# Second batch's first stage moved from the prologue into the unit loop

## The chip, the cores and the metric

The kernel runs on one core of one Trainium2 chip. The metric is the device time of one execution in microseconds. TensorE (PE in the rows) multiplies, VectorE (DVE), ScalarE (ACT) and GpSimd (POOL) work element by element, and SyncE (SP) issues most of the DMAs. Each engine takes its instructions strictly in the order of the program, and SP's queue does so too: a DMA that waits there holds back every DMA behind it.

## The reference

```python
def _attn_ref(x, w_r, w_i, b_r, b_i):            # x: 8 x 3072 x 256
    X = np.fft.rfft(x, axis=1)
    Yr = Xr @ w_r - Xi @ w_i + b_r
    Yi = Xr @ w_i + Xi @ w_r + b_i
    ...                                          # soft threshold by 0.01 of both
    return np.fft.irfft(Y, n=x.shape[1], axis=1)

def reference(**kwargs):
    x = _attn_ref(...).reshape(B * S, D)         # 24576 x 256
    x = _moe_ref(x, w_in, w_out)                 # relu(x @ w_in) ** 2 @ w_out
    return _moe2_ref(x, phi, w1, w2)             # 32 slots, 8 experts
```

The change touches the first part alone: the Fourier transform along the sequence, the complex product with the weights, the threshold and the way back.

## The kernel before

A sequence of 3072 is cut as 48 x 64, so that each transform becomes small matrix products. For each of the 8 batches there are two kinds of work.

The **first stage** of a batch is four blocks (`NA = 4`), numbered j over all batches: j = 0 to 3 are batch 0, j = 4 to 7 batch 1, and so on to 31. `a_mm(j, q)` (L214) multiplies two tiles of x (chunks 2j and 2j+1, each loaded by `load_x`, L204, in two DMAs of 192 KB) into four PSUM banks `psA`. `a_out` (L227, L232) copies one bank to SBUF, and after every second copy stores the result to a DRAM tensor `ad` of the batch in two DMAs. Copies not yet made stand in the list `done`.

The **units** are u = 0 to 95, twelve in each batch. `load_b(u)` (L239) reads rows of `ad` for units u and u+1 with two DMAs. As these rows cut across all blocks of the batch, the first one of a batch waits until every store of its four blocks has landed. Then come `b_mm` (`psB`, L247), the splits into high and low parts (`b_hi`, `b_lo`, `b_sum`), `l_mm` (`psL` and `psS`, L117 to L119, the weights' products), `l_move`, `l_relu`, `l_soft` on VectorE and ScalarE, and for two units together `c_mm` (`psC`, L331) and `c_out`, which stores to `zd`.

The units are software-pipelined by one loop over half units h: unit u's `b_mm` stands at h = 2u, its `l_mm` at h = 2(u+2), its `c_mm` at h = 2(u+4)+1. The function `starts(j)` gives the h at which block j's products are put in; at the other h one waiting `a_out` is made. At odd units `load_b(U+3)` is issued, so the first load of batch b stands at h = 24b - 5 and its first product at h = 24b.

Ahead of the loop stands the prologue: the loads of x for batch 0, the weights, the bias (`bias[0]`, read by `l_move`), block j = 0 to 3 and in this kernel one block more (`EX = 1`, j = 4), then 12 products on zeros (`busy1`, L503), `load_b(0)`, `load_b(2)` and the split of the weights. A decoder of weights that are stored in 64 bits (`decode`, L363 to L395) runs step by step from h = 17 on; each step of it on VectorE waits for a tile `raw` that SP has loaded.

At most eight DMAs of SP and ScalarE are on their way at once: each takes one of eight semaphores (DMAHW0 to 7) in turn, and waits for the DMA that had it before.

Of the kernel before, what the change touches and what calls it, by code (L numbers as in the profile page):

```python
# [25 lines left out]
DM = 256  # L26
NF = 16
TB = 8
NC = N2 // TB
# [74 lines left out]
def fft_moe_kernel(ctx, tc, x, w_r, w_i, b_r, b_i, moe_w_in, moe_w_out, moe2_phi, moe2_w1, moe2_w2,  # L104
                   c_f1, c_bm, c_cm, c_dm, c_st, out):
    nc = tc.nc
    NB = x.shape[0]
# [3 lines left out]
    NU = NP // 2  # L111
# [9 lines left out]
    def split(hi, lo, v, eng=None):  # L121
        nc.scalar.copy(hi, v)  # L122
        (eng or nc.vector).tensor_tensor(out=lo, in0=v, in1=f(hi), op=ALU.subtract)  # L123

    def drain(it):
        for _ in it:
            pass
# [31 lines left out]
    def early(tag, name):  # L159

        if tag.startswith("wia"):
            t = f(wpool.tile([128, 4, 2, 128], F32R, tag=tag, name=name).rearrange("p a b n -> p (a b n)"))
        else:
            t = wg[:, int(tag[2:])]
        return t.rearrange("p (a d) -> p a d", d=DM)
# [10 lines left out]
    bias = [k1p.tile([128, 2, DM], F32, tag=f"bias{j}", name=f"bias{j}") for j in range(2)]  # L176
# [7 lines left out]
    NA = N2 // 16  # L184
# [6 lines left out]
    def load_x(c):  # L191
        if c >= XL or c in xt:
            return
        b, k = divmod(c, NC)
        if c < NC:
            t = early(f"wia{c}", f"xt{c}")
        else:
            t = wka.tile([128, TX, DM], F32, tag="xt", name=f"xt{c}", bufs=XB)
        xv = x[b].rearrange("(n1 n2) d -> n1 n2 d", n2=N2)
        m = TX // 2 if c == 0 else TX  # L200
        for o in range(0, TX, m):
            for r in range(2):
                n = 16 * (k // 2) + 8 * r + 4 * (k % 2) + o
                nc.sync.dma_start(t[64 * r:64 * r + N1, o:o + m], xv[:, n:n + m])  # L204
        xt[c] = t

    def a_mm(j, q):
        b = j // NA
        if b not in ad:
            ad[b] = dram.tile([N1, N2, DM], F32, tag="ad", name=f"ad{b}", bufs=3)  # L210
        ps = [pbank(f"psA{j}_{q}_{r}").rearrange("p (a d) -> p a d", a=2) for r in range(2)]
        for r in range(2):
            for c in range(2):
                nc.tensor.matmul(ps[r][64 * c:64 * c + 64], lhsT=f1t[64 * r:64 * r + N1],  # L214
                                 rhs=xt[2 * j + c][64 * r:64 * r + N1, 2 * q:2 * q + 2], start=True, stop=True)
        for r in range(2):
            pa[j, q, r] = ps[r]
        if q:
            xt.pop(2 * j)
            xt.pop(2 * j + 1)  # L220

    def a_out(j, q, r, copy):
        i = 2 * j + r
        b, k = divmod(i, 2 * NA)
        if q == 0:
            sa[i] = early(f"wo{k}", f"sa{i}") if b == 0 else wka.tile([128, TX, DM], F32, tag="sa", name=f"sa{i}")
        copy(sa[i][:, 2 * q:2 * q + 2], pa.pop((j, q, r)))  # L227
        if q:
            t = sa.pop(i)
            for c in range(2):  # L230
                n = 8 * k + 4 * c
                (nc.sync if b else nc.scalar).dma_start(out=ad[b][:, n:n + TX], in_=t[64 * c:64 * c + N1])  # L232

    def load_b(u):
        b, k = divmod(u, NU)
        t = wkb.tile([128, 4, DM], F32, tag="bt", name=f"bt{u}")
        for ch in range(2):
            r = NP * ch + 2 * k
            nc.sync.dma_start(t[N2 * ch:N2 * ch + N2], ad[b][r:r + 4].rearrange("q n d -> n q d"))  # L239
        bt[u], bt[u + 1] = t[:, :2], t[:, 2:]  # L240
# [248 lines left out]
    with tc.manual_schedule():  # L489
# [17 lines left out]
        for c in range(NC):  # L507
            load_x(c)

        EX = 1 if NB > 1 else 0  # L510
        wr, wi, wn = (wkb.tile([128, 2, DM], F32, tag="ub", name=s, bufs=4) for s in ("wr", "wi", "wn"))
        for t, v in zip((wr, wi), (w_r, w_i)):
            nc.sync.dma_start(t, v.rearrange("(a p) n -> p a n", p=128))
        for k, v in enumerate((b_r, b_i)):
            nc.sync.dma_start(bias[0][:, k], v.rearrange("(o n) -> o n", o=1).broadcast_to([128, DM]))
        for c in range(NC, NC + 2 * EX):
            load_x(c)
        nc.sync.dma_start(bm[:, :4], c_bm[:, :4])
        wm = wkb.tile([128, 4, DM], F32, tag="sc", name="wm", bufs=1)[:, :2]

        def copy(j):
            return nc.scalar.copy if j % 2 else nc.vector.tensor_copy

        done = []

        def evacuate(n):
            for _ in range(n):
                k = done.pop(0)
                a_out(*k, copy(len(done)))

        for j in range(NA + EX):
            for q in range(2):
                a_mm(j, q)
                if done:
                    evacuate(2)
                done += [(j, q, r) for r in range(2)]
            if j == NA - 1:
                evacuate(2)
# [2 lines left out]
        nc.vector.memset(zero, 0.0)  # L541
        for t in (d0h, d0l):
            nc.vector.tensor_copy(t, zero[:, :, 0, :].broadcast_to([128, 2, 128]))
        if EX:
            evacuate(2)
            load_x(NC + 2)
        load_b(2)
        if EX:
            load_x(NC + 3)
        nc.sync.dma_start(bm[:, 4:8], c_bm[:, 4:8])  # L550
        nc.vector.scalar_tensor_tensor(out=wn, in0=wr, scalar=-1.0, in1=wi, op0=ALU.mult, op1=ALU.subtract)
        nc.vector.tensor_tensor(out=wm, in0=wi, in1=wr, op=ALU.subtract)
        for j, t in enumerate((wr, wn, wm)):
            split(lwh[j], lwl[j], t)
        nc.vector.tensor_copy(bias[1], bias[0])
        nc.vector.tensor_copy(bias[1][0:1, 1], bias[0][0:1, 0])
        dec_run = decode()
        aj = NA + EX
        if NB > 1:
            load_x(12)  # L560
            load_x(13)
        NT = NB * NU
        YL = 16 if NB > 1 else -5
        ylead = None
# [2 lines left out]
        def at(u, *steps):  # L567
            if 0 <= u < NT:
                for g in steps:
                    g(u)  # L570

        def starts(j):
            j -= NA + EX
            return 5 * j if j < 3 else 16 + 6 * (j - 3)

        for h in range(2 * NT + 12):
            U, o = divmod(h, 2)

            def first_stage():
                nonlocal aj  # L580
                if aj < NB * NA and h == starts(aj):
                    for q in range(2):
                        a_mm(aj, q)
                        done.extend((aj, q, r) for r in range(2))
                    load_x(2 * aj + 4)
                    load_x(2 * aj + 5)
                    aj += 1
                elif done:
                    a_out(*done.pop(0), nc.scalar.copy)

            if o == 0:
                at(U, b_mm)
                at(U - 2, l_mm)
                at(U - 4, l_soft)
                at(U - 1, b_lo)
                at(U - 5, c_out)
                first_stage()
                at(U - 3, l_relu)
            else:
                at(U - 4, c_mm)  # L600
                at(U - 2, l_move)
                at(U, b_hi)
                at(U - 1, lambda u: b_sum(u, nc.gpsimd))
                first_stage()
                if U % 2 and U + 3 < NT:
                    load_b(U + 3)

            if h % 4 == 2 and h < 18:
                nc.sync.dma_start(bm[:, h + 6:h + 10], c_bm[:, h + 6:h + 10])
            if h % 4 == 1 and h < 24:  # L610
                nc.sync.dma_start(cm[:, h // 2:h // 2 + 2], c_cm[:, h // 2:h // 2 + 2])
            if h == 8:
                next(dec_run)
            if h == 14:
                nc.sync.dma_start(ident, c_st[:, 0])
                nc.sync.dma_start(dmt, c_dm)
                nc.sync.dma_start(phi, moe2_phi.rearrange("(a p) n -> p a n", p=128))
                nc.vector.memset(ss, 0.0)
                nc.vector.memset(nm[0], 3.0e38)
            if h == 16:  # L620
                weight_tiles()
            if h > 16:
                for _ in range(1 + (h % 4 == 0)):
                    next(dec_run, None)
            if U == NT - YL and o == 1:
                drain(dec_run)
                wkax.close()
                zp = wgt.enter_context(tc.tile_pool(name="zp", bufs=1, reuse_waits="tile"))
                yp[0] = ypx.enter_context(tc.tile_pool(name="yp0", bufs=1, reuse_waits="tile"))
                ylead = stage_d(0, pbank, nc.vector)  # L630
            if ylead is not None and U > NT - YL + 1:
                next(ylead, None)
# [32 lines left out]
        o = OY + GR  # L665
# [396 lines left out]
        for n in range(NF):  # L1062
            c = n % 4
# [14 lines left out]
    with ExitStack() as p3, tc.manual_schedule():  # L1078
# [96 lines left out]
        for b in range(NB):  # L1175
            ob = out_tiles(b)
            for q in range(NQ):
# [6 lines left out]
                for h in range(2 if first else 1):  # L1184
                    for g in range(4):
                        o, i = (ob[q][:, 4 * h + g], pf[g][:, h]) if first else (ob[q][:, g::4], pf[g])
# [37 lines left out]
```

## Time and profile before

| | us |
|---|---|
| median of 3 runs | 2131.01 (2128.51 to 2131.42) |
| the profiled execution | 2138.45 |
| its span | 2136.7 |
| TensorE busy in the span | 2067.8 (97%) |
| VectorE, ScalarE, GpSimd busy | 1530.6, 1272.8, 1327.5 |
| first product of unit 0 (`psB`) | 41.68 |
| first product of unit 12, the first of batch 1 | 109.19 |
| last `psB` of the units | 519.6 |

The span is the time from the first to the last instruction that the profile shows. A busy TensorE is not TensorE at its peak, since the ends of its products are modelled. The Fourier part takes the first quarter of the span; all that the change touches lies there.

### The profile page before, as it was taken

The numbers are of one execution on the slowest core, as the hardware profiler recorded it, in microseconds if no ns is written. First come the engines' busy times: TensorE is split into PE (matmuls) and PEld (weight loads), VectorE is DVE, ScalarE is ACT, GpSimd is POOL, SyncE is SP. The second block draws the span as 40 slices with busy tenths as digits, with TensorE's granted clock in tenths as the row PEclk, the third lists the DMA queues.
The fourth block names the chain that finished last, engine by engine and source line by source line (L and its number), as shares of the span: only waits on it lengthen the run. The fifth ranks groups of instructions, "written<-read, shape, count | busy, mean of one in ns | idle before, by whom it ended". The sixth has DMA issues, their size and how long they took to land.

```text
span 2136.7 us, 55389 instructions
## 1 busy us (share of the span) xinstructions
PE 2067.8 (97%) x22288; PEld 1617.6 (76%) x22288; DVE 1530.6 (72%) x2591; ACT 1272.8 (60%) x2910; POOL 1327.5 (62%) x1583
## 2 busy tenths in 40 slices
PE   7999999999799999999999999999999999999994
PEld 3788788888677777777777777777777777777743
DVE  2666776778377777777777777777777777777743
ACT  2577667765466665666665666666566666556632
POOL 0234333421577788887778888778888777888500
PEclk7999999999899999999999999999999999999995
DMA  8999898863211111111111121111111111111589
GB/s 237 250 233 240 221 240 235 246 174 95 46 27 28 29 35 29 33 37 28 28 35 29 29 43 27 28 28 37 29 30 40 27 28 33 32 29 47 172 311 400
DMA packets 113484, 209.75 MB, mean 98 GB/s; under 512 B 14060, under 2 KB 80620, under 8 KB 106956
## 3 DMA queue, kind: packets, MB, share of 16 engines
q1 hardware_dynamic: 112060, 203.04, 35.3%
q8 instruction: 175, 2.87, 0.6%
q10 hardware_dynamic: 1168, 3.18, 0.4%
q14 instruction: 81, 0.66, 0.1%
HBM read 122.38 MB, written 83.79 MB: 96 GB/s over the span
## 4 chain that ended last, share of the span: by engine, by line
PE 88%; DMA 5%; ACT 2%; DVE 1%; POOL 1%; issue 1%; SPq 1%; ACTq 0%; DVEq 0%; POOLq 0%
PE psX L701 20%; PE psA L701 19%; PE ls L754 9%; PE psZ L701 6%; PE pz_a L765 5%; PE psB L247 4%; PE psC L331 4%; PE psY L459 3%; PE pz L765 3%; PE psA L214 3%; PE pz_x L765 2%; PE psL L117 2%; PE psL L118 2%; PE psL L119 2%; DMA out_dram<-ob 2%; PE psS L119 1%
## 5 line engine op out<-in xcount | busy, mean ns | idle before, releaser
L743 POOL TENSOR_TENSOR wg<-wg 128x384 f32<-128x384 f32 x797 | 716.6, 923 | 318.6 <-ACT wg L739 317.3
L747 DVE STREAM_TRANSPOSE gt<-wg 128x768 f32<-128x768 f32 x512 | 491.2, 964 | 135.9 <-POOL wg L743 133.8
L739 ACT ACTIVATE wg<-psX 128x384 f32<-128x384 f32 x512 | 251.7, 492 | 233.7 <-PE psX L701 195.9
L701 PE MATMUL psX<-yh,wia 128*128 128x384 f32 x1024 | 358.2, 350 | 9.8 <-DVE wg L735 6.9
L701 PE MATMUL psA<-yh,wia 128*128 128x384 f32 x1024 | 362.8, 359 | 0.0
L739 ACT ACTIVATE wg<-wg 128x384 f32<-128x384 f32 x512 | 267.3, 522 | 122.2 <-DVE wg L735 122.1
L701 PEld LDWEIGHTS psA<-yh,wia 128*128 128x128 f32 x1024 | 192.6, 188 | 103.4 <-DVE wg L735 57.6
L123 POOL TENSOR_TENSOR Sl<-Sf,Sh 128x256 fp32r<-128x256 f32 x96 | 75.5, 786 | 275.7 <-ACT Sh L122 245.6
L701 PEld LDWEIGHTS psX<-yh,wia 128*128 128x128 f32 x1024 | 192.5, 188 | 47.0 <-DVE acc L770 19.4
L754 PE MATMUL ls<-wg 128*32 128x384 f32 x2048 | 219.6, 499 | 0.3 <-DVE wg L743 0.3
L765 PE MATMUL pz_x<-gt,wg 32*32 32x512 f32 x1584 | 204.2, 598 | 0.0
L765 PE MATMUL pz<-gt,wg 32*32 32x512 f32 x2976 | 199.9, 598 | 0.0
L708 ACT COPY psX<-psA 128x384 f32<-128x384 f32 x256 | 120.0, 469 | 122.1 <-PE psA L701 121.3
L765 PE MATMUL pz_a<-gt,wg 32*32 32x512 f32 x1584 | 191.8, 594 | 0.0
L743 DVE TENSOR_TENSOR wg<-wg 128x384 f32<-128x384 f32 x227 | 182.3, 804 | 7.1 <-ACT wg L739 6.9
L735 DVE TENSOR_TENSOR wg<-psA,wg 128x384 f32<-128x384 f32 x256 | 135.7, 530 | 62.5 <-PE psA L701 62.3
L701 PE MATMUL psA<-yl,wia 128*128 128x384 f32 x512 | 172.6, 337 | 0.0
L701 PE MATMUL psZ<-yh,wib 128*128 128x384 f32 x512 | 172.5, 337 | 0.0
L701 PE MATMUL psX<-yh,wib 128*128 128x384 f32 x512 | 171.8, 336 | 0.0
L701 PE MATMUL psX<-yl,wia 128*128 128x384 f32 x512 | 171.7, 335 | 0.0
L701 PE MATMUL psA<-yh,wib 128*128 128x384 f32 x512 | 171.7, 335 | 0.0
L735 DVE TENSOR_TENSOR wg<-psX,wg 128x384 f32<-128x384 f32 x256 | 136.2, 532 | 41.8 <-ACT wg L722 29.9
(212 smaller groups left out, 4778.3 us busy)
## 6 DMA issues: line engine op xcount, KB each, us to landing
bt<-ad SPq DMA_DIRECT2D x96, 256.0 KB
zd<-sc SPq DMA_DIRECT2D x96, 256.0 KB
zt<-zd SPq DMA_DIRECT2D x64, 384.0 KB
xt<-in_x_dram SPq DMA_DIRECT2D x126, 192.0 KB
ad<-sa SPq DMA_DIRECT2D x112, 192.0 KB
out_dram<-ob SPq DMA_DIRECT2D x21, 1024.0 KB
wg<-ed SPq DMA_DIRECT2D x124, 96.0 KB
w<-in_moe_w_dram SPq DMA_DIRECT2D x5, 1024.0 KB
```

Source lines behind the costliest of these rows:

```text
L119: nc.tensor.matmul(o, lhsT=al, rhs=bh, start=False, stop=stop)
L123: (eng or nc.vector).tensor_tensor(out=lo, in0=v, in1=f(hi), op=ALU.subtract)
L247: nc.tensor.matmul(p[:, dh, :, l], lhsT=t[:, l, 128 * dh:128 * dh + 128], rhs=bm[:, 2 * (u % NU) + l], start=True, stop=True)
L331: nc.tensor.matmul(ps[l][:, v], lhsT=cm[w, (u - 1 + v) % NU, c], rhs=ub[v][w, c], start=c == 0, stop=c == 1)
L701: nc.tensor.matmul(p, lhsT=w[:, k, l], rhs=r[:, j], start=start and n == 0, stop=n == 2, skip_group_check=True)
L708: nc.scalar.copy(self.x, self.a)
L735: nc.vector.tensor_tensor(out=self.part(k), in0=p, in1=self.z, op=ALU.add)
L739: nc.scalar.activation(out=t, in_=t if p is None else p, func=AF.Relu)
L743: eng.tensor_tensor(out=t, in0=t, in1=t, op=ALU.mult)
L747: nc.vector.transpose(gt[:, 2 * self.q + a + window(self.s)], self.g[a])
L754: nc.tensor.matmul(lgp[o:o + 32], lhsT=pw[:, 2 * self.q + a], rhs=self.part(k), start=self.first, stop=self.last, skip_group_check=True)
L765: nc.tensor.matmul(ps[a][32 * c:32 * c + 32], lhsT=ee[w, c, k], rhs=gt[w, o:o + NT2, 32 * j:32 * j + 32], start=k == 0, stop=k == NB6 - 1, ...
```

## The change

Block j = 4 leaves the prologue: its x chunks 8 and 9, its products, copies and stores stand in the loop now, at h = 4. Batch 1's blocks start at h = 4, 8, 12 and 16 (before: the prologue, 0, 5 and 10), those of a later batch b at h = 24(b-2) plus 22, 28, 34 and 38 (before: plus 16, 22, 28 and 34). The bias and the x chunks 8 to 11 are loaded behind `load_b(0)` and `load_b(2)`, and the copy into `bias[1]` is made at h = 4. While batch 1's blocks are in work, up to two waiting copies are made at one h, some of them on VectorE.

```diff
-        EX = 1 if NB > 1 else 0
...
-        for k, v in enumerate((b_r, b_i)):
-            nc.sync.dma_start(bias[0][:, k], v.rearrange("(o n) -> o n", o=1).broadcast_to([128, DM]))
-        for c in range(NC, NC + 2 * EX):
-            load_x(c)
         nc.sync.dma_start(bm[:, :4], c_bm[:, :4])
...
-        for j in range(NA + EX):
+        for j in range(NA):
             for q in range(2):
                 a_mm(j, q)
...
-        if EX:
-            evacuate(2)
-            load_x(NC + 2)
         load_b(2)
-        if EX:
-            load_x(NC + 3)
         nc.sync.dma_start(bm[:, 4:8], c_bm[:, 4:8])
+        for k, v in enumerate((b_r, b_i)):
+            nc.sync.dma_start(bias[0][:, k], v.rearrange("(o n) -> o n", o=1).broadcast_to([128, DM]))
...
-        nc.vector.tensor_copy(bias[1], bias[0])
-        nc.vector.tensor_copy(bias[1][0:1, 1], bias[0][0:1, 0])
         dec_run = decode()
-        aj = NA + EX
-        if NB > 1:
-            load_x(12)
-            load_x(13)
+        aj = NA
+        for c in range(NC, NC + 4):
+            load_x(c)
...
         def starts(j):
-            j -= NA + EX
-            return 5 * j if j < 3 else 16 + 6 * (j - 3)
+            b, k = divmod(j, NA)
+            return 4 + 4 * k if b == 1 else 2 * NU * (b - 2) + (22, 28, 34, 38)[k]
...
                 elif done:
+                    if aj < 2 * NA and len(done) > 4:
+                        a_out(*done.pop(0), nc.vector.tensor_copy)
                     a_out(*done.pop(0), nc.scalar.copy)
+                    if aj == 2 * NA and len(done) > 1:
+                        a_out(*done.pop(0), nc.scalar.copy)
...
+            if h == 4:
+                nc.vector.tensor_copy(bias[1], bias[0])
+                nc.vector.tensor_copy(bias[1][0:1, 1], bias[0][0:1, 0])
```

On TensorE, at the end of the prologue, the kernel before has these rows (`psA` with `xt_287` and `xt_293` is block j = 5, the three `psB` are units 0, 1 and 2):

```order
L503 MATMUL busy_262<-idle 128x256 x12
L247 MATMUL psB_313<-bm,bt_275 128x2x64 x4
L214 MATMUL psA_0_0_318<-xt_287,f1t 64x512
L214 MATMUL psA_0_0_318<-xt_293,f1t 64x512
L214 MATMUL psA_0_1_319<-xt_287,f1t 64x512
L214 MATMUL psA_0_1_319<-xt_293,f1t 64x512
L214 MATMUL psA_1_0_324<-xt_287,f1t 64x512
L214 MATMUL psA_1_0_324<-xt_293,f1t 64x512
L214 MATMUL psA_1_1_325<-xt_287,f1t 64x512
L214 MATMUL psA_1_1_325<-xt_293,f1t 64x512
L247 MATMUL psB_343<-bm,bt_275 128x2x64 x4
L247 MATMUL psB_376<-bm,bt_290 128x2x64 x4
```

and the changed kernel these (`psA_356` is block j = 4, on chunks 8 and 9; left out are the other products of unit 0 and of this block):

```order
L503 MATMUL busy_237<-idle 128x256 x12
L247 MATMUL psB_282<-bm,bt_250 128x2x64 x4
L247 MATMUL psB_292<-bm,bt_250 128x2x64 x4
L247 MATMUL psB_320<-bm,bt_256 128x2x64 x4
L117 MATMUL psL_325<-lwh_89,Xh_287 128x256
...
L119 MATMUL psS_344<-lwh_88,Sl_314 128x256
L214 MATMUL psA_0_0_356<-xt_270,f1t 64x512
L214 MATMUL psA_0_0_356<-xt_273,f1t 64x512
L214 MATMUL psA_0_1_357<-xt_270,f1t 64x512
...
L214 MATMUL psA_1_1_363<-xt_273,f1t 64x512
L247 MATMUL psB_390<-bm,bt_256 128x2x64 x4
```

The products of units 0, 1 and 2 and the weights' products of unit 0 stand next to each other now; the block between units 0 and 1 is gone, and block 4 has come to stand behind the weights' products of unit 0.

On SP's queue, from the loads of the weights on, the kernel before has these rows (xt8 to xt11 are batch 1's first chunks, bt0 and bt2 are `load_b(0)` and `load_b(2)`):

```order
L513 DMA wr_149<-in_w_r_dram 128x2x256
L513 DMA wi_150<-in_w_i_dram 128x2x256
L515 DMA bias0_94<-in_b_r_dram 128x256
L515 DMA bias0_94<-in_b_i_dram 128x256
L204 DMA xt8_156<-in_x_dram 48x1024 x2
L204 DMA xt9_159<-in_x_dram 48x1024 x2
L518 DMA bm_86<-in_c_bm_dram 128x512
L239 DMA bt0_275<-ad0_164 64x4x256 x2
L232 DMA ad1_245<-sa8_258 48x1024 x2
L232 DMA ad1_245<-sa9_260 48x1024 x2
L204 DMA xt10_287<-in_x_dram 48x1024 x2
L239 DMA bt2_290<-ad0_164 64x4x256 x2
```

and the changed kernel these:

```order
L512 DMA wr_149<-in_w_r_dram 128x2x256
L512 DMA wi_150<-in_w_i_dram 128x2x256
L513 DMA bm_86<-in_c_bm_dram 128x512
L239 DMA bt0_250<-ad0_156 64x4x256 x2
L239 DMA bt2_256<-ad0_156 64x4x256 x2
L540 DMA bm_86<-in_c_bm_dram 128x512
L542 DMA bias0_94<-in_b_r_dram 128x256
L542 DMA bias0_94<-in_b_i_dram 128x256
L204 DMA xt8_270<-in_x_dram 48x1024 x2
L204 DMA xt9_273<-in_x_dram 48x1024 x2
L204 DMA xt10_276<-in_x_dram 48x1024 x2
L204 DMA xt11_279<-in_x_dram 48x1024 x2
```

`load_b(0)` and `load_b(2)` have moved ahead of the bias and of all chunks of batch 1, and the stores of block 4 (ad1) are no longer between them.

At the boundary to batch 1, SP's queue of the kernel before has these rows, with the semaphores waited for (sa16 and sa17 are already batch 2's, bt12 is `load_b(12)`):

```order
L363 DMA raw1_828<-in_moe_w_in_dram 128x512 [waits DMAHW2_49]
L232 DMA ad2_777<-sa16_825 48x1024 [waits DMAHW3_49,Activation_49]
L232 DMA ad2_777<-sa16_825 48x1024 [waits DMAHW4_49]
L239 DMA bt12_898<-ad1_245 64x4x256 [waits DMAHW5_49,PE_49]
L239 DMA bt12_898<-ad1_245 64x4x256 [waits DMAHW6_49]
L345 DMA zd0_63<-sc5_933 64x4x256 [waits DMAHW7_49,Activation_49]
L345 DMA zd0_63<-sc5_933 64x4x256 [waits DMAHW0_49]
L232 DMA ad2_777<-sa17_867 48x1024 [waits DMAHW1_49,Activation_49]
```

and the changed kernel these (sa14 and sa15 are batch 1's last):

```order
L232 DMA ad1_355<-sa14_796 48x1024 [waits DMAHW3_49,Activation_49]
L232 DMA ad1_355<-sa14_796 48x1024 [waits DMAHW4_49]
L232 DMA ad1_355<-sa15_838 48x1024 [waits DMAHW5_49,Activation_49]
L232 DMA ad1_355<-sa15_838 48x1024 [waits DMAHW6_49]
L239 DMA bt12_872<-ad1_355 64x4x256 [waits DMAHW5_49,DMAHW4_49,DMAHW6_49,DMAHW3_49,DMAHW7_49,DMAHW0_49,PE_49]
L239 DMA bt12_872<-ad1_355 64x4x256
L345 DMA zd0_63<-sc5_907 64x4x256 [waits DMAHW1_49,Activation_49]
```

The last stores of batch 1 stand right ahead of the first load that reads them now, and that load waits for their landing; the same order stands at the first loads of batches 2 to 7.

## Rows read from the trace of the kernel before

**Rows 1.** Busy time by stretch: us, busy us and instructions by engine, granted clock, DMA share, GB/s.
```profile
17.00:38.00 21.00, 17.47 (x49) 5.55 (x42) 6.78 (x13) 4.67 (x8) 0.00 (x0) 0.51 0.78 251
38.00:48.00 10.00, 7.49 (x40) 4.88 (x39) 3.14 (x12) 1.45 (x3) 0.00 (x0) 1.00 1.02 246
...
55.00:97.00 42.00, 41.12 (x343) 34.79 (x342) 25.83 (x46) 24.68 (x53) 7.80 (x10) 1.00 1.03 270
97.00:109.20 12.20, 9.52 (x41) 4.80 (x40) 6.85 (x14) 4.46 (x11) 5.48 (x9) 0.59 0.58 175
```

**Rows 2.** Timeline of SP's DMA queue, 18 to 42 us: start us, us until issued.
```profile
20.37 1.23 SPq L515 DMA_DIRECT2D bias<-in_b_r_dram  x1
21.65 1.24 SPq L515 DMA_DIRECT2D bias<-in_b_i_dram  x1
22.93 2.62 SPq L204 DMA_DIRECT2D xt<-in_x_dram  x4
...
33.58 1.35 SPq L239 DMA_DIRECT2D bt<-ad  x2
...
40.41 1.07 SPq L204 DMA_DIRECT2D xt<-in_x_dram  x2
```

**Rows 3.** Timeline of ScalarE's engine and queue, 18 to 36 us.
```profile
24.45 5.30 ACTq L232 DMA_DIRECT2D ad<-wg  x4
```

**Rows 4.** Timeline of TensorE, 16 to 30 us.
```profile
16.74 8.70 PE L214 MATMUL psA<-xt,f1t 48*64 48x512 f32 x26 [0.62 <-DMA xt<-in_x_dram]
```

**Rows 5.** Timeline of TensorE, 34 to 50.5 us.
```profile
35.08 6.77 PE L503 MATMUL busy<-idle 128*128 128x256 f32 x24
41.68 1.05 PE L247 MATMUL psB<-bm,bt 128*128 128x128 f32 x8
...
50.16 0.58 PE L247 MATMUL psB<-bm,bt 128*128 128x128 f32 x1
```

**Rows 6.** Timeline of TensorE, 61 to 63.5 us.
```profile
62.19 1.06 PE L247 MATMUL psB<-bm,bt 128*128 128x128 f32 x8
```

**Rows 7.** Timeline of TensorE, 94 to 110 us.
```profile
94.76 1.05 PE L247 MATMUL psB<-bm,bt 128*128 128x128 f32 x8
...
101.85 3.69 PE L214 MATMUL psA<-xt,f1t 48*64 48x512 f32 x16
105.48 3.78 PE L331 MATMUL psC<-ub,cm 64*128 64x256 f32 x16
109.19 1.05 PE L247 MATMUL psB<-bm,bt 128*128 128x128 f32 x6
```

**Rows 8.** Timeline of VectorE, 88 to 99 us.
```profile
96.95 0.29 DVE L382 TENSOR_SCALAR ex<-raw 128x256 int32<-128x256 int32 x1 [3.65 <-DMA raw<-in_moe_w_in_dram]
```

**Rows 9.** Chain of work that ended last, 86 to 112 us: start us, us, what.
```profile
89.67 7.18 DMA raw<-in_moe_w_in_dram
```

**Rows 10.** The same chain, 110 to 131 us.
```profile
121.46 1.88 PE psA L214 x16
...
126.56 1.93 PE psC L331 x16
```

**Rows 11.** Timeline of SP's queue, 153 to 170 us.
```profile
157.69 1.29 SPq L232 DMA_DIRECT2D ad<-sa  x2
159.07 1.28 SPq L239 DMA_DIRECT2D bt<-ad  x2
```

**Rows 12.** Timeline of ScalarE, 153 to 170 us.
```profile
157.06 0.60 ACT L227 COPY sa<-psA 128x512 f32<-128x512 f32 x1
```

**Rows 13.** Timeline of TensorE, 161 to 170 us.
```profile
161.78 1.05 PE L247 MATMUL psB<-bm,bt 128*128 128x128 f32 x8
...
168.70 1.16 PE L247 MATMUL psB<-bm,bt 128*128 128x128 f32 x8
```

**Rows 14.** The chain of work, 190 to 290 us.
```profile
257.40 3.49 DMA raw<-in_moe_w_out_dram
```

**Rows 15.** DMA issues of 0 to 530 us: engine, operation, count, KB each.
```profile
xt<-in_x_dram SPq DMA_DIRECT2D x126, 192.0 KB
```

## The prediction

> **What bounds the kernel now.** I read the busy time by stretch first. From 55 to 97 us TensorE is busy 41.12 of 42 us at the full clock, and the DMA engines are full as well: share 1.03, 270 GB/s [rows 1]. So the first twelve units run with two bounds close together. In a stretch where TensorE paces, a block of the first stage (`psA`) adds 1.88 us to the chain and a `psC` pair 1.93 us [rows 10]; a block moved into the loop costs its 1.88 us there, and is no longer free.
>
> Ahead of that TensorE is mostly not the bound. From 17 to 38 us its clock is granted at 0.51, the 1.2 GHz level, while DMA moves 251 GB/s [rows 1]. The timelines tell what is waited for. The last block of batch 0 ends its products at 16.74 + 8.70 = 25.44 us [rows 4]. Its four stores, which ScalarE issues, take from 24.45 to 29.75 us to be issued at all [rows 3], as the bias and the chunks 8 and 9 were issued at 20.37 to 25.55 us and fill the eight places. `load_b(0)` waits for these stores and goes out at 33.58 us [rows 2]. Behind block 4, TensorE then works through the 12 products on zeros from 35.08 to 41.85 us, and `psB` of unit 0 starts at 41.68 [rows 5]. `psB` of unit 1 reads the same tile, but block 5 stands ahead of it, whose chunk 11 is issued only at 40.41 us [rows 2]; unit 1 starts at 50.16 us [rows 5], 8.48 us after unit 0. Unit 4 starts at 62.19 [rows 6].
>
> Then one large stall: at unit 11 VectorE sits for 3.65 us in front of a decoder step [rows 8], whose `raw` took 7.18 us from issue to landing [rows 9]. TensorE runs dry, its clock falls to 0.59 of full for the stretch [rows 1], and a block takes 3.69 us instead of 1.88, a `psC` pair 3.78 instead of 1.93 [rows 7, 10]. From unit 11 (94.76) to unit 12 (109.19) pass 14.43 us [rows 7]. From unit 23 (161.78) to unit 24 (168.70), with the same work of one block and one `psC` pair, pass 6.92 us [rows 13]. The stall costs 7.5 us.
>
> **The change, step by step.**
>
> *Fewer bytes ahead of load_b(0).* Two chunks and the bias leave: four DMAs of 192 KB [rows 15] and two of 128 KB (128 x 256 floats), 1.05 MB. At 251 GB/s [rows 1] that is 4.2 us. I take `load_b(0)` at 33.58 - 4.2 = 29.4 us. From below nothing could be gained if the stores were late on their own, but their products end at 25.44 us [rows 4] and a landing takes 3.49 to 7.18 us [rows 14, 9], so 29 to 33 us bounds it; with the queue emptier, the lower end is nearer.
>
> *Unit 0.* Its data land some 4 us later (3.49 is the shortest row [rows 14]), at 33.4. The products on zeros start when the last copy out of PSUM is made, some 0.60 us [rows 12] behind 25.44, and last 6.77 us [rows 5], to 32.8: they no longer stand in the way. Unit 0 at 33.5 instead of 41.68, a gain of 8.2 us. Unit 1 follows directly, no block stands between: 34.6 instead of 50.16.
>
> *Units 2 to 4.* What is late next is SP's queue. Between `load_b(0)` and the landing of bt4 stand bt0, bt2 and bt4 (1.57 MB), the bias (0.26), three pieces of constants (0.79) and the chunks 8 to 11 (1.57): 4.19 MB, at 251 GB/s 16.7 us, so bt4 is there at 46.1 us. TensorE's order from unit 1 to unit 4 is the same as before (units 1 and 2, the weights' products of unit 0, one block, unit 3, the products of unit 1), and that took 62.19 - 50.16 = 12.0 us: 34.6 + 12.0 = 46.6. I take the later, 46.6 us, a gain of 15.6 us. By the same count of bytes the bias lands near 36 and chunk 9 near 39 us; `l_move` and block 4, which need them, come some 7 us behind unit 1. If the chunk came later, TensorE would stand for the difference.
>
> *Unit 4 to unit 12.* Before, this took 109.19 - 62.19 = 47.0 us with three blocks in it (7, 8, 9). Now four lie in it (5, 6, 7, 8): 47.0 + 1.9 = 48.9. I leave the stall at the decoder's step in: the load of `raw` stands, as before, right behind the chunks loaded at h = 16, now with two stores more ahead of it. Unit 12 comes at 46.6 + 48.9 = 95.5 us. The DMA engines allow it, barely: behind bt4 until bt12, 32 pieces of 192 KB and 21 of 256 KB stand on SP's queue (counted in the order), with small ones 11.9 MB. At 270 GB/s that is 44.1 us, at 246 (38 to 48 us [rows 1]) 48.4 us, so 90.2 to 94.5, counted from 46.1. The gain at unit 12 is 109.19 - 95.5 = 13.7 us.
>
> *Behind unit 12* the changed kernel has 23 blocks to do and the one before 22: a loss of 1.9 us. The additional copies are 0.60 us each on ScalarE [rows 12] and lie beside TensorE (ScalarE is busy 24.68 of 42 us, VectorE 25.83 [rows 1]); two of them at one h would cost 0.6 us where that cover is gone.
>
> *The first load of each batch.* Before, its stores had long landed. Now the last of them is issued in the same half unit and SP stands until it has landed; `zd` stores, x chunks and `raw` wait behind. No row shows this wait. The nearest: at the boundary to batch 2 ScalarE makes a copy at 157.06 [rows 12] in the place that the last one has in the changed kernel, its stores go out at 157.69 and the load at 159.07 [rows 11], and unit 24 starts at 168.70 [rows 13]. So 11.0 us are there for two landings, 0.4 us for the second store's issue and 0.65 for the first load's. With the shortest landing, 3.49 [rows 14], that needs 8.0 us and leaves 3.0; with the longest, 7.18 [rows 9], it needs 15.4 and lacks 4.4 us. Outside of the full stretch I take about 5 us, which just fits, and set 1 us for the seven boundaries together, and 1 us for one decoder load that stands right behind such a load (batch 5). Range: 0 to 7 x 4.4.
>
> On this wait the Trainium skill has a rule against the change: "DMA: Bandwidth & Descriptors", in its section on the anatomy of one DMA, says that the semaphore fires only when the last byte is confirmed in the target memory, that this receipt is most of a fixed cost of about 2 us, and heaviest for DRAM. By that figure, and the page's 436 GB/s beside it (both for the software path; SP's is the hardware one), a 192 KB store and a 256 KB load take an estimated 2.5 and 2.6 us with nothing else on the way; the boundaries would cost nothing, and the sum would be 2120.2. The shortest row here, 3.49 us, is longer; the sum goes by the rows.
>
> *Sum.* -13.7 + 1.9 + 1 + 1 = -9.8 us. The profiled execution took 2138.45 us, 7.4 more than the median of 2131.01; the difference carries over: 2128.6 for it, **2121.2 us** for the median.
>
> **The rivals.**
>
> *The stall at unit 11 goes too.* If `raw` lands in time, another 7.5 us go: 2113.7. For it: chunks 20 to 23 are asked for later now, so fewer bytes have been asked for by then. Against: x chunks stand right ahead of it as before, and two stores with them. 0.13.
>
> *DMA sets unit 12.* x chunks wait in SP's queue for the block that frees their tile, so the queue may not be able to move 270 GB/s closer to the start. Then only the bytes taken away ahead of unit 0 count: 4.2 - 1.9 = 2.3 us, 2128.7. For it: share 1.03 [rows 1]. Against: before, SP let the engines run at share 0.78 from 17 to 38 us and 0.58 from 97 to 109 [rows 1]. 0.15.
>
> *load_b(0) does not come earlier.* If the last four stores are late by themselves and not for the bytes ahead of them, the 4.2 us fall away and all else follows as reckoned: 2125.4. For it: nothing in the trace shows them alone. Against: all four could be issued by 26.1 us, and took until 29.75 [rows 3]. 0.11.
>
> *Slower: the batch boundaries.* Where both landings take over 5 us, TensorE stands at each of seven boundaries, and its clock falls as at 97 us, where block and `psC` together took 3.7 us more [rows 7, 10]. This decides from (9.8 + 1) / 7 = 1.5 us a boundary on. At 3 us it is 21 - 10.8 = 10.2 us slower, 2141.2; at 4.4 + 3.7 each it would be 46 us slower. For it: DMA is well loaded, and SP's queue has nothing to overtake with. Against: the 11 us above. The page's rule on the receipt works to this end, and here it would add up to those two landings. 0.09.
>
> **How the numbers follow.** The forecast, with 2115 to 2126 of its own, has 0.52; the others as given. 2112 to 2130 holds the forecast, the rival without the stall almost whole, the late stores and two thirds of the DMA rival: some 0.85. A measurement of this kernel can tell about 0.2% from no change, 4.3 us, so faster means below 2126.7: 0.52 + 0.13 + 0.09 of the late stores = 0.74; within: 0.15 + 0.02 = 0.17; slower: 0.09.
>
> **What the profile of the changed kernel would show.** `load_b(0)` issued near 29 us, unit 0 near 33.5, unit 1 within 2 us of it, unit 4 near 46.6 and unit 12 near 95.5 us; block 4 right behind unit 0's weights' products, without a wait for its chunk. At the boundaries, SP's `bt` waits 3 to 5 us for `ad`, and TensorE's `psB` of units 12, 24, ... starts without idle time ahead. From unit 12 to the last `psB` it should take 410.4 us (519.6 - 109.2) plus 1.9 to 4. Wrong would be: unit 4 early and unit 12 late (DMA); a VectorE that waits for `raw` at several boundaries; TensorE at half clock there.

## The result, and the profile of the changed kernel

The changed kernel takes 2151.47 us (median, 2150.68 to 2152.94), the one before 2130.75 beside it on the same chip: ratio 1.010, 95% interval 1.0082 to 1.0117. It is 20.7 us, or 1%, slower; 2121.2 was predicted.

The profiled execution took 2151.23 us. The head of its page (busy us, share of the span, instructions):

```profile
span 2149.4 us, 55378 instructions
...
PE 2063.0 (96%) x22288; PEld 1619.4 (75%) x22288; DVE 1537.5 (72%) x2591; ACT 1269.7 (59%) x2910; POOL 1321.6 (61%) x1583
```

The prologue does what was predicted. SP's queue and TensorE's timeline of the changed kernel (start us, us; in brackets the idle time before and what ended it) answer to [rows 2, 5, 6]:

```profile
28.79 2.67 SPq L239 DMA_DIRECT2D bt<-ad  x4
```

```profile
33.74 5.46 PE L247 MATMUL psB<-bm,bt 128*128 128x128 f32 x24 [5.52 <-DMA bt<-ad]
...
41.99 2.09 PE L214 MATMUL psA<-xt,f1t 48*64 48x512 f32 x16
...
49.87 2.04 PE L247 MATMUL psB<-bm,bt 128*128 128x128 f32 x8 [2.58 <-DMA bt<-ad]
```

`load_b(0)` goes out at 28.79 instead of 33.58 us, the 24 products of units 0, 1 and 2 stand in one row from 33.74 on, block 4 runs at 41.99 without a wait, and unit 4 starts at 49.87 instead of 62.19. At this point the change is 12.3 us ahead.

Against before_again, a second execution of the kernel before (next section), it is 11.3 us ahead there (61.2). All of it is gone by unit 12. Busy time by stretch of the changed kernel (us, busy us and instructions of PE, PEld, DVE, ACT, POOL; granted clock, DMA share, GB/s), which answers to [rows 1]:

```profile
28.80:38.00 9.20, 4.26 (x20) 4.29 (x21) 1.25 (x4) 1.33 (x3) 0.00 (x0) 0.69 0.87 211
...
64.00:82.00 18.00, 15.36 (x85) 11.16 (x84) 6.83 (x13) 7.07 (x15) 1.46 (x2) 0.72 0.70 195
...
94.00:109.70 15.70, 10.70 (x68) 8.04 (x66) 9.21 (x18) 10.22 (x24) 7.26 (x12) 0.78 0.63 191
```

From 64 to 82 us TensorE stands 2.6 us (before it was busy nearly all the time there [rows 1]), is granted 0.72 of its full clock (part of the stretch at 1.2 GHz), and the DMA engines are only 70% busy. Neither of the two bounds of the prediction is at work there. The waits of ScalarE from 28 to 112 us (engine, line, what it waited for: us in total, times, longest) name a third, first in the changed kernel, then the same line in the one before:

```profile
ACT sa L227 <- DMA ad<-sa: 25.8, 4, 9.5
```

```profile
ACT sa L227 <- DMA ad<-sa: 1.9, 1, 1.9
```

The copies out of PSUM wait for the stores that read the tile `sa` before. The pool `wka` has **two** `sa` tiles, and a block fills both: `sa8` and `sa9` are block 4's, `sa10` and `sa11` block 5's. The timelines of ScalarE, SP and TensorE in the changed kernel show one such wait whole:

```profile
55.62 0.59 ACT L227 COPY sa<-psA 128x512 f32<-128x512 f32 x1 [0.75 <-PE psA L214]
64.42 0.58 ACT L227 COPY sa<-psA 128x512 f32<-128x512 f32 x1 [8.22 <-DMA ad<-sa]
...
80.90 0.59 ACT L227 COPY sa<-psA 128x512 f32<-128x512 f32 x1 [9.54 <-DMA ad<-sa]
...
95.45 1.07 ACT L227 COPY sa<-psA 128x512 f32<-128x512 f32 x2 [7.80 <-DMA ad<-sa]
```

```profile
56.44 2.11 SPq L204 DMA_DIRECT2D xt<-in_x_dram  x4
58.60 0.42 SPq L363 DMA_DIRECT2D raw<-in_moe_w_in_dram  x1
59.12 0.84 SPq L232 DMA_DIRECT2D ad<-sa  x2
```

```profile
66.73 0.58 PE L117 MATMUL psS<-lwh,Sh 128*128 128x256 f32 x1 [2.62 <-ACT Sh L122]
68.69 3.69 PE L214 MATMUL psA<-xt,f1t 48*64 48x512 f32 x16
...
99.17 0.58 PE L117 MATMUL psS<-lwh,Sh 128*128 128x256 f32 x1 [4.89 <-ACT Sh L122]
```

At h = 9 the last copy of block 4 (into `sa9`, on VectorE) and the first of block 5 (into `sa10`, ScalarE at 55.62) are made together. At h = 10 ScalarE is to fill `sa11`, which is `sa9`'s tile. But the store of `sa9` stands on SP's queue behind four x loads, which in turn waited for block 5's products; it goes out at 59.12 to 59.96 and has landed at 64.4 (the DMA engines are 0.96 busy in that time). ScalarE stands for 8.22 us, and behind the copy wait its `Xh` and `Sh`. TensorE runs dry for 2.62 us and falls to the lower clock, so that block 6 takes 3.69 us instead of 1.88 [rows 10]. The pattern repeats once in each of the next two blocks, with 9.54 and 7.80 us; TensorE stands for 1.17 us at the second and 4.89 us at the third.

So unit 12 starts at 109.69 us, no earlier than before [rows 7]. The times at which `psB` of some units starts, read from TensorE's records of the profiled executions, with the kernels of the next section:

| kernel | unit 0 | 4 | 12 | 48 | 60 | 72 | 95 | span |
|---|---|---|---|---|---|---|---|---|
| before, as in the rows | 41.7 | 62.2 | 109.2 | 295.1 | 355.4 | 415.9 | 518.8 | 2136.7 |
| before_again | 41.9 | 61.2 | 103.0 | 291.0 | 350.8 | 411.3 | 514.2 | 2132.3 |
| changed | 33.7 | 49.9 | 109.7 | 295.5 | 362.6 | 423.1 | 533.4 | 2149.4 |
| after_raw3 | 33.5 | 50.4 | 110.8 | 295.7 | 356.4 | 417.5 | 525.5 | 2143.2 |
| after_sa5 | 32.5 | 48.3 | 98.6 | 286.2 | 349.8 | 410.6 | 524.5 | 2140.3 |
| after_sa5_late2_raw3 | 33.5 | 49.1 | 95.3 | 283.5 | 343.6 | 404.7 | 507.7 | 2124.7 |
| quick_sa5_late2_raw3 | 33.3 | 49.9 | 95.1 | 283.2 | 343.3 | 404.4 | 507.4 | 2126.7 |
| before_new_late_2 | 40.8 | 59.9 | 98.4 | 289.1 | 355.8 | 415.9 | 528.6 | 2147.8 |
| before_raw3 | 42.4 | 63.2 | 102.8 | 285.5 | 345.6 | 406.8 | 509.7 | 2124.8 |

The second half of the loss lies in two places behind unit 12. From unit 48 to 60 the changed kernel needs 67.1 us, before_again 59.8; from unit 72 to 95 110.3 against 102.9, where 1.9 of the 7.4 us are one block more (three instead of two from unit 72 to 84). Both are batch boundaries. The chain of work of the changed kernel at the first of them (start us, us, what) answers to [rows 9]:

```profile
346.57 2.68 DMA ad<-sa
349.37 0.60 SPq L239
350.02 0.61 SPq L239
350.72 5.24 DMA raw<-in_moe_w_out_dram
356.05 0.29 DVE ex L382
...
358.34 4.37 PE psC L331 x16
```

SP stands until batch 5's last stores have landed, and the decoder's `raw` behind `load_b(60)` is issued only then. VectorE waits for it, TensorE stands for 5.09 us up to 358.34 and does `psC` at half its clock (4.37 us; 1.93 in [rows 10]). At the second place a tile `zt` of the next stage's load (`load_z`, L444) waits in the same queue, right behind `load_b(84)`:

```profile
479.99 0.17 SPq L444
480.21 7.84 DMA zt<-zd
488.04 0.14 issue
488.18 1.14 PE psY L459 x60
```

TensorE stands for 2.1 us in all in front of `psY`, the product that reads `zt`, and is granted 0.72 of its full clock behind it, from 488 to 494 us (`psB` takes 1.64 instead of 1.16 us).

### The profile page after: what moved, and what is told of

Its sections match the earlier page's. It is cut to its first block, busy times and chain, and to the rows that moved or that the text cites. A ratio compares the mean times of both kernels' runs of the same rounds, so it can differ in the third digit from the quotient of the medians.

```text
span 2149.4 us, 55378 instructions
## 1 busy us (share of the span) xinstructions
PE 2063.0 (96%) x22288; PEld 1619.4 (75%) x22288; DVE 1537.5 (72%) x2591; ACT 1269.7 (59%) x2910; POOL 1321.6 (61%) x1583
## 4 chain that ended last, share of the span: by engine, by line
PE 85%; DMA 5%; issue 3%; ACT 3%; POOL 2%; DVE 1%; SPq 0%; ACTq 0%; DVEq 0%; POOLq 0%
PE psX L697 20%; PE psA L697 19%; PE ls L750 9%; PE psZ L697 6%; PE pz_a L761 4%; PE psC L331 3%; PE psB L247 3%; PE psY L459 3%; PE pz L761 3%; PE pz_x L761 2%; PE psA L214 2%; DMA out_dram<-ob 2%; PE psL L117 2%; PE psL L119 2%; PE psL L118 2%
## 5 line engine op out<-in xcount | busy, mean ns | idle before, releaser
L739 DVE TENSOR_TENSOR wg<-wg 128x384 f32<-128x384 f32 x227 | 189.7, 836 | 4.8 <-ACT wg L735 4.6
```

The costliest lines, as they stand in the source:

```text
L739: eng.tensor_tensor(out=t, in0=t, in1=t, op=ALU.mult)
```

## The experiments

My theory after the two traces: **three waits**, each made by a store's landing. (1) Batch 1's copies wait for the stores of two `sa` tiles. (2) `raw` is asked for one step ahead only, behind first loads that wait now. (3) The late places put the first load of each later batch right behind its stores. Rival: the loss is one thing, the DMA engines, and the waits only show it. Ratios are to the kernel before, run beside each kernel on the same chip; 0.001 is 2.1 us.

**The kernel before, again.** 

> The kernel before, unchanged, for a second trace. Its first profiled execution took 7.7 us more than the median of the others. If the wait for raw ahead of unit 12 (7.5 us) belongs to that one execution, the new trace lacks it: span near 2129 us, unit 12 near 102 us. If it stands in every execution, the new span is again 2135 us or more and unit 12 comes at 107 to 110 us. Timed: within 0.2% of itself.

2134.82 us, ratio 1.0011 (0.9999 to 1.0023). It matters for its trace: unit 12 starts at 103.0 instead of 109.2 us. The wait at unit 11 is there again, but shorter: TensorE stands for 1.41 us, where it stood for 2.66 in the first execution. The row of the first execution, then those of the second:

```profile
99.89 0.58 PE L117 MATMUL psS<-lwh,Sh 128*128 128x256 f32 x1 [2.66 <-ACT Sh L122]
```

```profile
97.69 0.38 PE L117 MATMUL psS<-lwh,Sh 128*128 128x256 f32 x1 [1.41 <-ACT Sh L122]
...
99.17 1.95 PE L214 MATMUL psA<-xt,f1t 48*64 48x512 f32 x16
101.04 2.00 PE L331 MATMUL psC<-ub,cm 64*128 64x256 f32 x16
```

The block and the `psC` pair behind it run at the full clock, in 3.95 us; in [rows 7] they took 7.47. So the stall of [rows 7 to 9] belongs for the most part to that one execution: from unit 11 to 12 pass 9.2 us instead of 14.4. With before_again as the base the changed kernel is 6.7 us behind at unit 12 and loses another 12.5 up to unit 95 (423.7 against 411.2). Of these 19.2 us 2.1 come back behind the units: the two spans differ by 17.1.

**Five store tiles.** The `sa` of batches 1 and later take five slices that lie unused then.

```diff
-            sa[i] = early(f"wo{k}", f"sa{i}") if b == 0 else wka.tile([128, TX, DM], F32, tag="sa", name=f"sa{i}")
+            sa[i] = early(f"wo{k if b == 0 else 1 + i % 5}", f"sa{i}")
```

> The changed kernel with five buffers instead of two for the copies of the first stage. Theory A (a copy has to wait until the store that read its buffer has landed, and ScalarE with all its work stands behind it): the three waits of 8.2, 9.5 and 7.8 us at batch 1 go, unit 12 comes near 95 us instead of 109.7, and the time falls by 14 to 20 us, to 2132 to 2138. Theory B (the DMA engines cannot bring batch 1 earlier, whoever waits): unit 12 stays at 105 us or later, and the time at 2148 to 2152.

2142.07 us, 1.0048 (1.0035 to 1.006), 11 us less by the ratios; neither range held it. The wait of the copies for stores has left ScalarE's list (these traces call the store tiles `wg`), and unit 12 starts at 98.6 instead of 109.7 us. Its stretches beside those of the changed kernel:

```profile
64.00:84.00 20.00, 20.00 (x169) 17.30 (x168) 11.94 (x23) 12.06 (x26) 4.11 (x5) 1.00 0.99 285
84.00:98.60 14.60, 9.95 (x45) 5.24 (x43) 6.89 (x14) 4.45 (x11) 5.47 (x9) 0.66 0.68 209
```

Up to 84 us TensorE is full at the full clock, and the DMA engines move 285 GB/s instead of 195: in the changed kernel they had not been the bound. Then the decoder stalls it, as its chain shows:

```profile
79.79 0.71 SPq L604
80.54 5.68 DMA raw<-in_moe_w_in_dram
86.32 0.29 DVE ex L382
```

TensorE stands for 4.64 us behind it. Whether the places four half units apart or the second copy at one h does more to fill a tile too early was not run apart.

**The old places from batch 4 on**, batch 3's in between.

```diff
-            return 4 + 4 * k if b == 1 else 2 * NU * (b - 2) + (22, 28, 34, 38)[k]
+            return 4 + 4 * k if b == 1 else 2 * NU * (b - 2) + ((22, 28, 34, 38) if b == 2 else (20, 26, 30, 34) if b == 3 else (16, 22, 28, 34))[k]
```

> The changed kernel, with the blocks of batches 4 to 7 at their old places (16, 22, 28, 34) and those of batch 3 between the two; batches 1 and 2 as in the changed kernel. If the load right behind its last store costs time at the later boundaries, the stall ahead of unit 60 (15.0 us from unit 59 to 60, 6.9 without it) goes, and the time falls by 6 to 11 us, to 2141 to 2146. If all of the loss lies in batch 1, it stays at 2150 to 2153.

2154.71 us, 1.0109 (1.0093 to 1.0126): a miss, above both ranges. The stall that was named goes (from unit 59 to 60 pass 8.2 us), and from unit 60 to 95 it gives back 7.5 us (163.3 against 170.8). But batch 3's blocks, two pairs of them four half units apart, wait for two `sa` tiles as batch 1's do:

```profile
ACT sa L227 <- DMA ad<-sa: 10.4, 4, 4.9
```

(ScalarE, 160 to 260 us; 2.9, 1, 2.9 in the changed kernel). Units 24 to 36 take 78.1 instead of 63.9 us. **With five store tiles besides** the same places:

> Both edits together: five buffers, and old places from batch 4 on. Theory A: both savings add up, 2122 to 2130 us, below the kernel before. Theory B: what the late places give alone, 2141 to 2146.

2137.65 us, 1.003 (1.0018 to 1.0041), 3.8 us less than five tiles alone by the ratios, and between the two ranges. Units 24 to 36 still take 70.6 us: the store tiles explain 7.5 of the 14.2 us lost there, a fifth block in this stretch 1.9, and the rest stays open.

**The late places alone**, in the kernel before with its own prologue, run twice; the stretches are read from the second run.

```diff
-            j -= NA + EX
-            return 5 * j if j < 3 else 16 + 6 * (j - 3)
+            b, k = divmod(j, NA)
+            return 5 * (k - 1) if b == 1 else 2 * NU * (b - 2) + (22, 28, 34, 38)[k]
```

> The kernel before with its prologue and batch 1 untouched; only the blocks of batches 2 to 7 stand at the new places (22, 28, 34, 38). If the loads right behind the last stores cost time (seven boundaries, the load of zt behind the last of them), 8 to 14 us slower than before, 2140 to 2146, with unit 12 at 100 to 104 us as before. If all of the loss of the change lies in batch 1, within 0.2% of before, 2128 to 2136.

2143.29 us, 1.0054 (1.0033 to 1.0074).

> The kernel before with its own prologue, and the change's places for the blocks of batches 2 and later alone (22, 28, 34, 38). Theory (the first load of a batch behind its last stores holds up SP's queue, and raw, zd and the last weights' tile zt with it): unit 12 within 3 us of 103 us as in the kernel before, the loss comes behind unit 24, above all from unit 48 to 60 (a decoder load behind the boundary) and from unit 72 to 95; 2140 to 2146. Rival (the late places cost nothing and the earlier loss was a chance of the run): 2130 to 2134.

2142.45 us, 1.0042 (1.0028 to 1.0056). This half of the change costs 9 to 12 us by itself, at the places that were named: units 48 to 60 take 66.7 us and 72 to 95 112.7, against 59.8 and 102.9 (the profiled execution, 2149.62 us, lost more than the median). Unit 12 comes at 98.4, earlier than expected: one block less stands ahead of it. The chain at the boundary repeats the changed kernel's:

```profile
339.95 2.65 DMA ad<-sa
342.72 0.60 SPq L239
343.37 0.61 SPq L239
344.07 5.54 DMA raw<-in_moe_w_out_dram
```

**A third `raw` tile.** Each is loaded two steps ahead.

```diff
-                t = dec.tile([128, W], I32 if wide else F32, tag="raw", name=f"raw{n}", bufs=2)
+                t = dec.tile([128, W], I32 if wide else F32, tag="raw", name=f"raw{n}", bufs=3)
...
+            load(1)
...
-            load(n + 1)
+            load(n + 2)
```

In the kernel before: 

> The kernel before with the same three buffers for raw alone: 3 to 7 us faster, 2125 to 2129, if the waits for raw that its traces show are on the path; no change if DMA sets the pace there.

2127.63 us, 0.9984 (0.9972 to 0.9996), 3.4 us less, as expected.

In the changed kernel alone: 

> The changed kernel with three raw tiles of the decoder instead of two, each loaded one step earlier; the store buffers sa stay two. Theory (the copies of batch 1 wait for the stores that read their two buffers): ScalarE still stands for some 20 us or more ahead of its copies up to 110 us, psB of unit 12 starts at 103 to 110 us, and only the decoder's share goes: 2142 to 2149. Rival (the decoder's late loads are what holds up batch 1, and ScalarE's waits cost nothing): unit 12 at 97 us or earlier as in the kernel that has both mends, 2133 to 2137.

2146.23 us, 1.0057 (1.0039 to 1.0074), 9 us less by the ratios. Unit 12 stays at 110.8, and ScalarE waits for the stores as long as ever:

```profile
ACT sa L227 <- DMA ad<-sa: 26.0, 3, 9.2
```

What it gains lies behind unit 48: units 48 to 60 take 60.7 us again. So causes (1) and (2) are two: each mend leaves the other's wait standing.

With five store tiles: 

> The changed kernel with five buffers for the copies and three for raw, each raw loaded one step of the decoder earlier. If what is left of the loss is VectorE in front of late raw tiles (4.6 us idle ahead of unit 12, 3.0 at unit 59, each with the clock down behind it), the time falls from 2142 to 2130 to 2136 and unit 12 comes at 90 to 94 us. If DMA sets unit 12, raw only lands earlier at the cost of others: 2139 to 2143.

2133.17 us, 1.0016 (1.0006 to 1.0027), as expected, but unit 12 comes at 97.1 us instead of 90 to 94.

**All three mended**, batch 2's blocks at 21, 26, 30, 34 and the later ones at the places of before (this run has five store tiles and three `raw` besides).

```diff
-            return 4 + 4 * k if b == 1 else 2 * NU * (b - 2) + (22, 28, 34, 38)[k]
+            return 4 + 4 * k if b == 1 else 2 * NU * (b - 2) + ((21, 26, 30, 34) if b == 2 else (16, 22, 28, 34))[k]
```

> The changed prologue and batch 1, five buffers, three for raw, and the blocks of batch 2 at 21, 26, 30, 34, of later batches at their old places 16, 22, 28, 34. If the prologue's gain is real and was lost to buffers, raw and boundaries, it shows here: unit 12 near 92 us, from there on as before with one block more, 2118 to 2126. If DMA takes it back, 2128 to 2134.

2127.56 us, 0.9986 (0.9975 to 0.9996), between the two expected ranges. Unit 12 starts at 95.3 us, but before_raw3, whose prologue is the old one, is as fast. One wait is left ahead of unit 12, on SP's queue and on TensorE:

```profile
83.85 2.43 SPq L232 DMA_DIRECT2D ad<-wg  x4
90.53 1.26 SPq L239 DMA_DIRECT2D bt<-ad  x2
```

```profile
95.35 1.13 PE L247 MATMUL psB<-bm,bt 128*128 128x128 f32 x8 [3.67 <-DMA bt<-ad]
```

Two kernels were to tell whether this is the boundary or the DMA engines. The first moves batch 1's blocks to 4, 8, 11, 14 and its last store to h = 17:

```diff
-            return 4 + 4 * k if b == 1 else ...
+            return (4, 8, 11, 14)[k] if b == 1 else ...
...
-                    if aj < 2 * NA and len(done) > 4:
+                    if aj <= 2 * NA and len(done) > 2 and h < 18:
```

> The kernel with five store buffers, three raw tiles and the batches' blocks from 2 on at their old places (batch 2's at 21, 26, 30, 34), and with batch 1's blocks at h = 4, 8, 11, 14 instead of 4, 8, 12, 16, the second copy made at any h below 18 while more than two wait, so that batch 1's last store is issued at h = 17 instead of 19. Theory (the 3.7 us of idle TensorE ahead of unit 12, and the half clock behind it, come from the first load of batch 1, which waits for stores issued in the same half unit): the idle time ahead of unit 12 falls below 1 us, unit 12 starts at 91 to 93 us, 2119 to 2125. Rival (the DMA engines set unit 12, whatever stands at the boundary): unit 12 at 94 us or later, 2126 to 2130.

2129.20 us, 0.9982 (0.9968 to 0.9995), as the rival had it, with unit 12 at 100.8 us in the profiled execution (2133.54 us). The x loads of batch 2 come earlier with the blocks: `load_b(10)` now stands behind four of them and goes out at 84.19 instead of 75.45 us, when one of them has landed (78.58, 5.60 us in the chain), and TensorE stands at unit 10 instead:

```profile
89.11 2.05 PE L247 MATMUL psB<-bm,bt 128*128 128x128 f32 x8 [3.43 <-DMA zd<-sc]
```

The second leaves blocks and x loads where they were and only makes the copies sooner:

```diff
-                    if aj < 2 * NA and len(done) > 4:
+                    if aj < 2 * NA and len(done) > 3 or h == 17 and len(done) > 3:
                         a_out(*done.pop(0), nc.vector.tensor_copy)
                     a_out(*done.pop(0), nc.scalar.copy)
-                    if aj == 2 * NA and len(done) > 1:
-                        a_out(*done.pop(0), nc.scalar.copy)
+                    while h == 17 and done:
+                        a_out(*done.pop(0), (nc.scalar.copy, nc.vector.tensor_copy)[len(done) % 2])
```

> The kernel with five store buffers, three raw tiles and the old places from batch 2 on (batch 2's at 21, 26, 30, 34), blocks and x loads of batch 1 where they were (4, 8, 12, 16), and only its copies made sooner: all that wait are made at h = 17, some of them on VectorE, so that batch 1's last store is issued two half units earlier, ahead of one constant and one raw. Theory (the 3.7 us of idle TensorE ahead of unit 12 is the first load of batch 1, waiting for its last stores): the idle time ahead of unit 12 falls below 1.5 us, unit 12 starts at 91 to 93.5 us, 2122 to 2126. Rival (the DMA engines set unit 12, whatever stands right ahead of its load): TensorE stands 2.5 us or more in units 8 to 12 as before, unit 12 at 94 us or later, 2126 to 2130.

2125.97 us, 0.9967 (0.9955 to 0.998): 0.33% faster than the kernel before and the fastest here, though its interval overlaps that of before_raw3. The idle time falls to 1.52 us, near what the theory had, yet unit 12 starts at 95.1, as the rival had it. SP's queue and the chain say why:

```profile
83.38 2.17 SPq L232 DMA_DIRECT2D ad<-wg  x4
85.60 1.11 SPq L605 DMA_DIRECT2D cm<-in_c_cm_dram  x1
86.76 0.71 SPq L363 DMA_DIRECT2D raw<-in_moe_w_out_dram  x1
90.07 1.26 SPq L239 DMA_DIRECT2D bt<-ad  x2
```

```profile
84.73 5.26 DMA ad<-wg
90.07 0.60 SPq L239
90.72 4.26 DMA bt<-ad
```

The last store goes out only 0.8 us sooner than in after_sa5_late2_raw3 (84.73 instead of 85.53), takes 5.26 us to land, and the load another 4.26, behind a stretch (64 to 82 us) in which the DMA engines move 302 GB/s at share 1.01; while that store lands (84.7 to 90.0 us) they move 307 at 0.94. The load goes out at 90.07 instead of 90.53. So the idle time fell mostly because TensorE came later (unit 11 at 88.4 instead of 86.5 us), which is no proof for the theory. Once the three waits are gone, DMA seems to come close to setting unit 12. How much of the last 1.5 us is order and how much transfer stays open; no kernel with fewer bytes was run.

By the ratios times 2131 us the loss is undone in four steps: 1.0100 to 1.0048 by the store tiles (11 us), to 1.0016 by the third `raw` (7), to 0.9986 by the earlier places (6), to 0.9967 by sooner copies (4). Each step is uncertain by some 3 us; the intervals of the last two kernels overlap, and their traces don't show the last step (unit 95 at 507.7 and 507.4 us). The third `raw` tile helps the kernel before too, so these kernels are to be set against before_raw3 at 0.9984: that the moved block gains anything beside it is not shown.

## Why the prediction was wrong

**Right: the prologue.** `load_b(0)` 28.79 us (29.4 predicted), unit 0 33.74 (33.5), unit 1 within 2 us of it, no wait at block 4. With 1.05 MB less ahead of it this load came 4.8 us earlier (4.2 reckoned), 3.8 us against before_again (32.60).

**Mis-sized: units 2 to 4.** 49.87 us instead of 46.6. The step was the right one, bt4 lands last (2.58 us of waiting for it), but the 4.19 MB ahead of its landing were counted at 251 GB/s, and from 28.8 to 38 us the engines moved 211, as the row of that stretch shows. That is 1.5 us by an estimate from the two rates; for the rest, the engines moved 4.8 MB up to 49.8 us (229 GB/s), 0.6 more than were counted, as DMAs issued behind bt4 (four x loads from 44.01 us on) were on their way beside it.

**Failed: "Unit 4 to unit 12".** This step is the main error: 59.8 us instead of 48.9, though 48.9 held the stall of the base; before_again took 41.8 us for it. I took the time of before and added one block, and let the additional copies, by the next step of the prediction, "lie beside TensorE" as 0.60 us each. I asked what the copies cost, not what they wait for. A block uses both `sa` tiles; before, its copies were made one at each half unit and blocks stood five apart, so that a tile was filled again three half units after its store. With blocks four apart and two copies at one h, `sa9` is filled at h = 9 and wanted again at h = 10. The pool's two buffers stand in the code, and [rows 14, 9] had landings, of `raw` loads, of 3.49 and 7.18 us. Unit 23 to 24 took 6.92 us with a block and a `psC` pair [rows 13], 3.5 for each half unit: one of them can't hold an issue behind four x loads and a landing. after_sa5 and after_raw3 show this cause from both sides. The sign that the prediction had named for the DMA rival, unit 4 early and unit 12 late, was seen, but the DMA engines were not the cause (share 0.70 from 64 to 82 us).

**Failed by size: "The first load of each batch".** 1 us for seven boundaries and 1 for the decoder load were set, 9 to 12 measured (the two runs of the late places alone). Most boundaries cost nothing, as reckoned: units 60 to 72 take 60.5 us in the changed kernel and in before_again, and from 110 us on no `psB` of the changed kernel waits for its `bt` (SP's longest wait there for a batch's stores is 3.2 us). The cost sits where something else stands behind the load on SP's queue, `raw` at unit 60 and `zt` at unit 84. The rival "slower: the batch boundaries" (0.09) had the sign and the mechanism of the queue that can't overtake; it spread the price over seven boundaries, where two paid, 7.3 us and, without the block more, 5.5. On these waits the Trainium skill ("DMA: Bandwidth & Descriptors", the anatomy of one DMA) says for the software path that a transfer's semaphore waits for the receipt of its last byte, most of a fixed cost of about 2 us. The estimate worked out from it, 2.5 us for such a store, agrees with the shortest store here, 2.65 us at 340 us in before_new_late_2 (DMA share 0.52 from 337 to 344 us), and is half of the 5.26 us that one takes at 84.73 in the last kernel (share 0.94).

**The stall of the base.** I left the 7.5 us at unit 11 in, for both kernels, and said that the profiled execution's excess carries over. It did not: before_again takes 5.2 us less from unit 11 to 12, so the excess of 7.4 us of the first execution was mostly this stall, and the changed kernel's profile (2151.23 us) has no such excess over its median.

**The sum.** For the profiled execution 2128.6 us was predicted and 2151.2 measured: 22.6 us off. Ahead of unit 12 it is 14.2 us (109.7 instead of 95.5), from there to unit 95 10.2 (423.7 instead of the 409.6 of before, 518.8 - 109.2, with 3.9 for a block and the boundaries), and behind the units some 1.8 come back. Against the median another 7.7 come from the base.

**DMA sets unit 12** (0.15) did not decide the changed kernel, whose engines are 0.70 busy from 64 to 82 us, but in the mended one it may be what takes back half of the gain. Against before_raw3, after_sa5_late2_raw3 is 14 us ahead at unit 4, 7.5 at unit 12, and behind it one block more and short waits take all but 2 of it.

## What to carry to other kernels

When work is moved closer together, count for each tile that a DMA reads how long it is from the issue of that DMA to the next write of the tile, the transfers ahead of it on the queue included, and set it against a landing time from a loaded stretch: a copy of 0.6 us made ScalarE stand for 8 to 10 us here. When a load is put right behind the stores that it reads, look for what stands behind it on the same queue; the load itself may be covered where a small transfer behind it isn't. And profile the base twice before a stall in it is used as a term.

## What the runs showed of the hardware

A DMA share near 1 is no fixed rate: 270 GB/s at share 1.03 [rows 1], 302 GB/s at 1.01 in the last kernel from 64 to 82 us. The landing of a 192 KB store took 2.65 us where the share was 0.52 and 5.26 where it was 0.94. Two executions of one program differed by 6.2 us at unit 12: in the one a 256 KB load took 7.18 us to land [rows 9] and TensorE stood for 2.66 us and went on at its lower clock (0.59 granted from 97 to 109.2 us [rows 1]), in the other the same load, issued at 89.57, was there by 94.75 us, TensorE stood for 1.41 us, and its clock stayed full.
